# Who issues the transfers: SyncE alone, or SyncE, ScalarE and GpSimd

## The chip, the core and the metric

The kernel runs on one core of a Trainium2 chip. A core has five engines with an instruction queue each: TensorE (PE in the profile; its weight loads are PEld), VectorE (DVE), ScalarE (ACT), GpSimd (POOL) and SyncE (SP). They share an on-chip memory of 128 partitions; matmul results go to a second one, PSUM, here used as four buffers p0 to p3. Transfers are issued from the queue of SyncE, ScalarE or GpSimd and are carried out by 16 DMA engines. Each queue is worked off in program order: an instruction that has to wait holds up all that stand behind it on the same engine.

The metric is the device time of one execution in microseconds (us). Before the change it is 249.68 us, the median of three runs (249.4 to 249.89).

## The reference, cut to what matters

Two layers, each of them a sequence mixer A (a long convolution over the sequence with a gate) and an MLP B. The mixer's kv and its convolution depend on k, v and the filter alone, so both layers use the same y, and the kernel computes it once.

```python
def _A_ref(q, k, v, shift_k, ssm_k, ssm_D):      # S = 2048, D = 512
    k_shift = ...                                # 4 taps along the sequence
    kv = k_shift * v
    y = irfft(rfft(kv, 2S) * rfft(ssm_k, 2S))[:S]  # long convolution
    y = y + kv * ssm_D
    return q * y

def _B_ref(x, w1, b1, w2, b2):                   # 512 -> 1376 -> 512
    return gelu(layernorm(x) @ w1 + b1) @ w2 + b2

x = A_q
x = x + _A_ref(layernorm(x), A_k, A_v, A_shift_k, A_ssm_k, A_ssm_D)
x = x + _B_ref(layernorm(x), B_w1, B_b1, B_w2, B_b2)
x = x + _A_ref(layernorm(x), A_k, A_v, ...)      # the second layer
x = x + _B_ref(layernorm(x), ...)
return x
```

## The kernel before: the parts that the change touches

The kernel is a list of pieces, and a table ORDER that says in which order they are emitted and on which engine each runs: `sw00.S` puts the piece sw00 on SyncE, `.A` is ScalarE, `.G` GpSimd, `.D` VectorE, `.P` TensorE; digits name the buffers taken. The order within an engine is the order in this table.

The convolution is done as matrix products on a two-step transform. K pieces transform the filter, kv pieces are the taps, U pieces the first transform step of kv, X the second, T the product with the filter's spectrum (on VectorE), V and Y the way back. Then come the gate, the layer norms and the MLPs (m1, ge, m2, ad), one group of tokens after the other.

The filter's spectrum lies in two copies, the second with the two halves of the partitions swapped. The half swaps (sw00, sw01, sw10, sw11: first digit the half of the features, second the half of the frequencies) write the second copy with two transfers each:

```python
def swap(it, off=off):                                   # line 421
    for a in range(2):
        queue(it).dma_start(at(KSW + off, [[1, 16 * 256]], a, 64, 2), at(off, [[1, 16 * 256]], 1 - a, 64, 2))
KX[f].append(add(f"sw{f}{j}", {"S": 1200}, deps, swap, dma=2700))
```

A product T reads both copies, so T00 and T01 need sw00, T02 and T03 need sw01, T20 and later ones sw10 and sw11:

```python
def mul(it, xe=xe, spec=spec):                           # line 513
    eng = nc.vector if it["eng"] == "D" else nc.gpsimd
    xb = view(xbb[xe["slot"]["xb"]], [8, CW])
    x2 = apf(xb, xb.offset, [list(xb.ap[0]), [0, 2], [CW, 8], [1, CW]])
    eng.tensor_tensor(spec(), x2, spec(), ALU.mult)      # line 517
tm = add(f"T{cc}{j}", {"D": 1140}, [xe, KX[cc // 2][j // 2]] + KW[cc // 2][2 * j:2 * j + 2], mul,
         free=[(xe, "xb")])
```

The loads and the transposes. A piece's queue follows from its letter; the transposes by DMA always go to SyncE:

```python
def queue(it):
    return {"S": nc.sync, "A": nc.scalar, "G": nc.gpsimd}[it["eng"]]

def load(name, dst, src, ns, deps=(), after=()):
    return add(name, {"S": 400, **QUEUE.get(name, {})}, deps, lambda it: queue(it).dma_start(dst, src), dma=ns, after=after)   # line 325

def ktload(ct):                                          # k, transposed: line 369
    return lambda it: nc.sync.dma_start_transpose(kT[:, ct, 16:16 + S], k_d[:, ct * P:ct * P + P])
lv = [load(f"lv{o}", uv[:, 8 * o:8 * o + 8, :], vd[:, 8 * o:8 * o + 8, :], 2650) for o in range(2)]
lW = load("lW", Wt[:], W_h.ap().bitcast(BF16), 2650)     # transform tables
lM = load("lM", Mt[:], M_h.ap().bitcast(BF16), 5300)
...
lx = load("lx", xr[:], qd[:, GT:NT, :], 4000, s1p)       # x of groups 1 to 3
w1 = load("w1", W1t[:], B_w1.rearrange("(ct p) f -> p ct f", p=P), 3600)

def w2load(it):                                          # lines 546 to 548
    queue(it).dma_start(W2t[:, 0:FT - 1, :], ...)
    queue(it).dma_start(W2t[0:FL, FT - 1, :], ...)
    queue(it).dma_start(W2t[FL:FL + 1, FT - 1, :], apf(B_b2, 0, [[D, 1], [1, D]]))
```

GpSimd computes the first layer norm's statistics of group 0 (piece pa00, lines 622 to 636; its scratch lies where W1 will be, so w1 waits for it), then the power -1/2 of them (pb0, lines 273 and 275). Later it applies that norm (pc00, pc01, line 284), sets a row of ones (ho, line 553) and computes more such powers.

TensorE has two groups of 28 matmuls on the identity: one at the start (`warm`, line 97) and one in a wait ahead of the MLP (`IDLE = (28, 0, 0)`, line 670).

Of the kernel before, what the change touches and what calls it, by code (L numbers as in the profile page):

```python
# [14 lines left out]

ORDER = """
warm.P dg.D lK1.S lK0.S lK3.S lv1.S lH.S lx0.S lk0.S KT1.P0 KT1e.D KT0.P1 K1S0.P2 KT0e.D K1S3.P3 K1S0e.A0 K1S2.P0
K1S3e.D K0S3.P1 K1S2e.A K0S0.P2 K0S0e.D1 K1S1.P3 K0S3e.A KT3.P0 K1S1e.A K0S1.P1 lv0.S KT3e.D K0S2.P2 pa00.G lK2.S
K0S1e.A K1T1.P3 lW.S K0S2e.D lM.S lk3.S K3S0.P0 K3S3.P1 K3S0e.A2 K1T1e.D K0T1.P2 K3S3e.A K3S1.P0 K0T1e.D K1T0.P3
K3S1e.A K0T0.P1 K1T0e.D kv0.P20 K0T0e.D K3S2.P3 kvm01.D KT2.P1 K3S2e.A kvm00.D K3T0.P3 KT2e.A U0S0.P0 K3T0e.D K3T1.P2  # L20
U0S0e.A3 K200.P1 K3T1e.D U0S1.P3 K200e.A K201.P0 U0S1e.D K205.P2 K201e.A U0S2.P1 K205e.A U0S2e.D K207.P3 K2S0.P0
K207e.A U0S3.P2 K2S0e.D4 K2S1.P1 lk1.S U0S3e.A K2S2.P3 K2S3.P0 K2S2e.D K2S1e.A U0T0.P2 K2S3e.A K202.P1 U0T0e.D5
K204.P3 K202e.A K2T1.P0 K204e.D K203.P2 lk2.S U0T1.P1 K2T1e.D K203e.A X00.P3 pb0.G U0T1e.D K2T0.P2 X00e.A0 K216.P0
K2T0e.D sw00.S K217.P1 K216e.A K214.P3 K217e.D K211.P2 K214e.A w1.S K215.P0 K211e.A K215e.D K210.P1 K206.P3 K210e.A
K212.P2 K206e.D sw11.S X01.P0 K212e.A X03.P1 X01e.D1 X02.P3 sw01.S X03e.A2 K213.P2 K213e.A T00.D kv2.P01 sw10.S T01.D
X02e.A0 kv1.P23 kvm21.D kvm20.D kvm11.D U2S0.P0 V00.P1 U2S0e.A6 kvm10.D V00e.A0 U2S3.P0 U2S3e.D U1S0.P2 U1S1.P3
U1S0e.A1 U1S2.P1 U1S1e.D U2S1.P0 U1S2e.A U1S3.P2 T02.D U2S2.P3 U1S3e.A V01.P1 U2S1e.D U2S2e.A U1T0.S2 V02.P2 V01e.D
kv3.P30 V02e.A U1T1.S T03.D V03.P1 kvm31.D pc00.G U2T0.S3 V03e.A kvm30.D X10.P2 X10e.A1 X11.P1 U3S1.P0 pc01.G X11e.A0
# [2 lines left out]
T21.D X22e.A2 X23.P0 X23e.A0 V11e.D V20.P1 V13e.A V21.P0 T22.D TP00.S6 V20e.A3 X30.P3 T23.D X31.P2 X30e.A1 V22.P1  # L31
X31e.D2 V21e.A V23.P3 TP01.S V22e.A T30.D X33.P0 X32.P2 V23e.A TP11.S T31.D Y00.P1 X32e.A0 V30.P3 Y00e.D TP02.S
X33e.A1 Y01.P2 T32.D V31.P1 Y01e.A TP12.S T33.D V30e.A4 V32.P0 V31e.A ga0.D V33.P2 TP21.S V32r.A Y02.P3 V32f.D ho.G
V33f.A gs0.D lx.S Y02e.A TP03.P1 TP30.S V33r.A ga1.D TP03e.A TP13.P0 TP23.P3 gs1.D TP13e.A Y03.P2 TP33.P1 gl0.D
TP23e.A Y11.P0 gl2.D gp0.G TP33e.A Y10.P3 gb0.D Y11e.A gp2.G gl1.D LT0.P1 TP20.S LT0e.A gb2.D gp1.G Y10e.A m10x0.P0
Y03e.D gb1.D pa10.D LT1.P1 ge0x0.A m10x1.P2 TP31.S LT2.P3 LT1e.D pa21.D m10y0.P1 TP32.S LT2e.A pa11.D ge0x1.A m10y1.P0
TP22.S ge0y0.A m10z0.P3 pa20.D w2.S pb1.G m10z1.P2 ge0y1.A pc10.D ge0z0.A pb2.G pc11.D m10z2.P1 pd10.D ge0z1.A Y30.P0
pd11.D ge0z2.A Y20.P3 Y21.P2 Y20e.A pe10.D Y31.P1 pc21.A m200.P3 pe11.D Y31e.A Y21e.A pa30.D pf1.G pc20.A pg11.D
pg10.A pd20.D lt11.S m201.P1 Y30e.A pd21.D lt10.S pe20.D pe21.D m110.P2 ad01.D pf2.G m111.P0 ge10.A pa31.D pg21.A
m112.P1 pg20.D pb3.G ge11.A pa41.D lt21.S m113.P2 ge12.A lt20.S pc30.D m114.P0 pc31.D ge13.A pd30.D m115.P1 ge14.A  # L40
# [751 lines left out]
```

## Time and profile before

| | |
|---|---|
| Time | 249.68 us (249.4 to 249.89) |
| Span of the profiled execution | 247.7 us |
| ScalarE's share, GpSimd's share | 59%, 20% |
| Moved by the DMA engines | 31.06 MB, 54778 packets |
| Of it on SyncE's queue (q1) | 30.68 MB, 49.5% of 16 engines' span |
| On ScalarE's queue (q10), on GpSimd's (q0) | 0.07 MB, 0.00 MB |
| Half swaps: issue to landing, min, median, max | 3.0, 7.2, 7.8 us |
| k transposes: issue to landing, min, median, max | 5.7, 10.9, 15.1 us |

How to read it: part 2 of the page cuts the span into 40 slices of 6.2 us, and a digit is the busy share of an engine in tenths. A row of a timeline has the start in us, the time taken in us, engine, line, operation, what is written and read, and a count; a q behind the engine's name means its queue, that is, the issue of a transfer and not its data. The time to issue is not the time to move: when a transfer has landed is told by the updates of its semaphore. In the names, low and high are the two large blocks of on-chip memory, so low<-low is a half swap, high<-tabM the table M, Wt<-tabW the table W.

### The profile page before, as it was taken

Reading aid. Unit: us, or ns where it says so; the run is one execution under the profiler, and the core shown is the slowest. Engines: PE = TensorE matmul, PEld = TensorE weight load, DVE = VectorE, ACT = ScalarE, POOL = GpSimd, SP = SyncE. Lnnn points to the kernel's source line nnn. Section 1 sums busy time; section 2 is a strip of 40 time slices with the busy share of each in tenths; the row PEclk is TensorE's granted clock in tenths of the full one; section 3 lists DMA queues with packets and bytes.
Section 4 is the critical chain, followed back from the end, with each engine's and each line's share of the span. In section 5 each row is a group of like instructions: output and inputs, shape, how many; then the busy total and the mean of one; then the engine's idle time right before and its main releaser. Section 6 shows DMA issues by size and latency. Waiting matters only on the chain.

```text
span 247.7 us, 4836 instructions
## 1 busy us (share of the span) xinstructions
PE 235.8 (95%) x1932; PEld 148.0 (60%) x1943; DVE 174.3 (70%) x343; ACT 147.0 (59%) x214; POOL 50.3 (20%) x79
## 2 busy tenths in 40 slices
PE   7999999998998889999999999999999999999994
PEld 6899798787897688444444444444444444444443
DVE  1898899998999899999978569759659410110232
ACT  2666979478999889947787464164275264064000
POOL 4089981103001214104030110110110100000000
PEclk9999999999999999999999999999999999999999
DMA  6999999959999996041304220500400330020111
GB/s 221 328 308 443 200 264 343 423 103 178 220 187 168 285 165 228 1 85 21 67 2 84 46 43 0 77 9 3 80 5 0 68 105 0 0 85 3 42 70 57
DMA packets 54778, 31.06 MB, mean 125 GB/s; under 512 B 49410, under 2 KB 51684, under 8 KB 53604
## 3 DMA queue, kind: packets, MB, share of 16 engines
q1 hardware_dynamic: 54002, 30.68, 49.5%
q8 instruction: 15, 0.25, 0.4%
q0 software_dynamic: 80, 0.00, 0.3%
q10 hardware_dynamic: 674, 0.07, 0.2%
q14 instruction: 7, 0.06, 0.1%
HBM read 12.40 MB, written 2.10 MB: 59 GB/s over the span
## 4 chain that ended last, share of the span: by engine, by line
PE 73%; DVE 12%; ACT 8%; DMA 4%; issue 2%; DVEq 0%; ACTq 0%
PE p_89 L748 10%; PE p_90 L748 9%; PE p_90 L722 8%; PE p_88 L722 8%; PE p_89 L722 8%; PE p_91 L748 7%; PE p_91 L722 6%; PE p_88 L748 5%; DVE low L336 3%; DMA ZT_83<-ZT_80 2%; PE p_88 L347 2%; DMA sT<-in_A_shift_k_dram 2%; ACT xb_84 L334 2%; DVE low L517 1%; PE p_91 L403 1%
## 5 line engine op out<-in xcount | busy, mean ns | idle before, releaser
L722 PEld LDWEIGHTS <-W1t 128*128 128x128 bf16 (+1 forms) x440 | 40.2, 100 | 37.5 <-issue 1.4
L748 PEld LDWEIGHTS <-low 128*128 128x128 bf16 (+1 forms) x363 | 35.4, 98 | 40.8
L748 PE MATMUL p_89<-low 128*128 128x512 bf16 (+3 forms) x119 | 25.9, 369 | 0.1
L733 ACT ACTIVATE low<-p_88,B_72 128x512 bf16<-128x512 f32 (+3 forms) x33 | 17.1, 588 | 14.8 <-PE p_89 L748 10.3
L756 DVE TENSOR_TENSOR high<-p_90,high 128x1024 bf16<-128x1024 f32 (+1 forms) x5 | 5.6, 1118 | 28.4 <-PE p_90 L748 28.4
L722 PE MATMUL p_88<-low,W1t 128*128 128x512 bf16 (+3 forms) x132 | 23.7, 326 | 0.7 <-ACT low L334 0.7
L733 ACT ACTIVATE low<-p_90,B_72 128x512 bf16<-128x512 f32 (+4 forms) x28 | 15.9, 639 | 11.7 <-PE p_90 L722 8.5
L722 PE MATMUL p_90<-low,W1t 128*128 128x512 bf16 (+4 forms) x112 | 22.7, 347 | 0.0
L748 PE MATMUL p_90<-low 128*128 128x512 bf16 (+1 forms) x95 | 22.0, 379 | 0.2
L733 ACT ACTIVATE low<-p_89,B_72 128x512 bf16<-128x512 f32 (+4 forms) x29 | 14.9, 593 | 11.8 <-PE p_91 L748 9.0
L722 PE MATMUL p_89<-low,W1t 128*128 128x512 bf16 (+4 forms) x116 | 20.6, 324 | 0.4 <-DVE low L336 0.4
L748 PE MATMUL p_91<-low 128*128 128x512 bf16 (+1 forms) x76 | 17.2, 379 | 0.1
L722 PE MATMUL p_91<-low,W1t 128*128 128x512 bf16 (+2 forms) x80 | 17.2, 358 | 0.0
L733 ACT ACTIVATE low<-p_91,B_72 128x512 bf16<-128x512 f32 (+2 forms) x20 | 11.8, 655 | 7.0 <-PE p_89 L748 3.1
L525 PEld LDWEIGHTS <-low 128*128 128x128 bf16 x256 | 15.0, 98 | 1.2 <-issue 0.7
L748 PE MATMUL p_88<-low 128*128 128x512 bf16 (+2 forms) x64 | 13.6, 361 | 0.1
L756 DVE TENSOR_TENSOR high<-p_89,high 128x1024 bf16<-128x1024 f32 (+1 forms) x5 | 5.3, 1062 | 9.3 <-PE p_89 L748 9.3
L606 DVE TENSOR_TENSOR high<-high 128x1024 bf16<-128x1024 bf16 (+1 forms) x16 | 10.7, 669 | 1.2 <-ACT high L286 1.1
L263 DVE BATCH_NORM_STATS2 lst_104<-high 128x6 f32<-128x512 bf16 x16 | 10.2, 682 | 0.1
L263 DVE BATCH_NORM_STATS2 lst_96<-high 128x6 f32<-128x512 bf16 x16 | 10.2, 680 | 0.0
L627 POOL TENSOR_TENSOR W1t<-W1t 128x512 f32<-128x512 f32 (+8 forms) x17 | 9.7, 568 | 1.3
L273 POOL TENSOR_TENSOR lrs_98<-lrs_98,mhalf 128x4 f32<-128x4 f32 x4 | 4.0, 1006 | 27.5 <-DVE lnm_99 L270 27.5
(227 smaller groups left out, 446.6 us busy)
## 6 DMA issues: line engine op xcount, KB each, us to landing
low<-low SPq DMA_DIRECT2D x8, 512.0 KB, 7.2
low<-in_A_ssm_k_dram SPq DMA_DIRECT2D x4, 512.0 KB, 5.0
high<-in_A_v_dram SPq DMA_DIRECT2D x2, 1024.0 KB, 7.5
high<-tabM SPq DMA_DIRECT2D x1, 2048.0 KB, 14.0
high<-in_A_q_dram SPq DMA_DIRECT2D x1, 1536.0 KB
W1t<-in_B_w_dram SPq DMA_DIRECT2D x1, 1376.0 KB
low<-in_B_w_dram SPq DMA_DIRECT2D x1, 1280.0 KB, 6.7
Wt<-tabW SPq DMA_DIRECT2D x1, 1024.0 KB, 8.4
```

What stands on the lines that cost most here:

```text
L263: nc.vector.bn_stats(self.st[:, i, h, :], xg(g, i, i + 1, c0, c9)[:, 0, :])
L273: nc.gpsimd.tensor_tensor(self.rs[:, a:b], self.rs[:, a:b], mhalf[:, a:b], ALU.pow)
L334: nc.scalar.activation(d, s, AF.Copy)
L336: nc.vector.tensor_copy(d, s)
L347: nc.tensor.matmul(o[:, i, :], src[:, 4 * q + i, cs], Ft[:], start=True, stop=not extra)
L525: nc.tensor.matmul(o[:, i, :], T[:, r, i, :], Mt[:, k0 + i, r, :], start=r == 0, stop=r == 1)
L606: nc.vector.tensor_tensor(tmp[:, a:b, c0:c9], ln[:, a:b, c0:c9], ys, ALU.mult)
L627: g_.tensor_tensor(d[:, :, 0:w], src[:, :, 0:w], src[:, :, w:2 * w], ALU.add)
L722: nc.tensor.matmul(o[0:m, ft - fts[0], :], W1t[:, ct, ft * P:ft * P + m], lnT[n % 3][:, a:b, ct, :], start=ct == 0, stop=ct == CT - 1)
L733: nc.scalar.activation(hT[n % 2][0:m, ft, a * P:b * P], psv(pe, dims)[0:m, ft - fts[0], :], AF.Gelu_apprx_tanh, bias=B1[0:m, ft:ft + 1])
L748: nc.tensor.matmul(o[:, i - a, 0:c9 - c0], hT[n % 2][0:m, ft, i * P:(i + 1) * P], W2t[0:m, ft, c0:c9], start=ft == 0, stop=ft == FT - 1)
L756: nc.vector.tensor_tensor(xs, psv(pe, [2, D])[:, 0:b - a, 0:c9 - c0], xs, ALU.add)
```

## The change

Nothing is computed differently and nothing is moved otherwise; only the queue from which some transfers are issued changes. In the table ORDER, v's second load half (lv0), W and M go from SyncE to ScalarE; the four half swaps (eight transfers), W1, x of groups 1 to 3 and W2 go from SyncE to GpSimd. All transposes by DMA, the other loads and the stores stay with SyncE. Both groups of identity matmuls are in both kernels. The aim is that SyncE, in whose queue the transposes stand, is not held up by plain transfers.

```diff
-K1S3e.D ... K1S1e.A K0S1.P1 lv0.S KT3e.D K0S2.P2 pa00.G lK2.S
-K0S1e.A K1T1.P3 lW.S K0S2e.D lM.S lk3.S K3S0.P0 ...
+K1S3e.D ... K1S1e.A K0S1.P1 lv0.A KT3e.D K0S2.P2 pa00.G lK2.S
+K0S1e.A K1T1.P3 lW.A K0S2e.D lM.A lk3.S K3S0.P0 ...
...
-K2T0e.D sw00.S K217.P1 K216e.A ... K214e.A w1.S K215.P0 ...
-K212.P2 K206e.D sw11.S X01.P0 ... X02.P3 sw01.S X03e.A2 K213.P2 K213e.A T00.D kv2.P01 sw10.S T01.D
+K2T0e.D sw00.G K217.P1 K216e.A ... K214e.A w1.G K215.P0 ...
+K212.P2 K206e.D sw11.G X01.P0 ... X02.P3 sw01.G X03e.A2 K213.P2 K213e.A T00.D kv2.P01 sw10.G T01.D
...
-V33f.A gs0.D lx.S Y02e.A TP03.P1 TP30.S ...
+V33f.A gs0.D lx.G Y02e.A TP03.P1 TP30.S ...
...
-TP22.S ge0y0.A m10z0.P3 pa20.D w2.S pb1.G ...
+TP22.S ge0y0.A m10z0.P3 pa20.D w2.G pb1.G ...
```

(Cut: the lines are shortened at the three dots; all letters that change are shown.) On GpSimd sw00 comes after pa00 and pb0, and w1, sw11, sw01 and sw10 follow it in this order, ahead of pc00; lx comes after ho, w2 ahead of pb1. On ScalarE lv0 comes after K1S1e, and lW and lM come after K0S1e, ahead of K3S0e.

More of the change, by code (lines that the diff above doesn't have):

```diff
@@ L17 @@
 warm.P dg.D lK1.S lK0.S lK3.S lv1.S lH.S lx0.S lk0.S KT1.P0 KT1e.D KT0.P1 K1S0.P2 KT0e.D K1S3.P3 K1S0e.A0 K1S2.P0
-K1S3e.D K0S3.P1 K1S2e.A K0S0.P2 K0S0e.D1 K1S1.P3 K0S3e.A KT3.P0 K1S1e.A K0S1.P1 lv0.S KT3e.D K0S2.P2 pa00.G lK2.S
-K0S1e.A K1T1.P3 lW.S K0S2e.D lM.S lk3.S K3S0.P0 K3S3.P1 K3S0e.A2 K1T1e.D K0T1.P2 K3S3e.A K3S1.P0 K0T1e.D K1T0.P3
+K1S3e.D K0S3.P1 K1S2e.A K0S0.P2 K0S0e.D1 K1S1.P3 K0S3e.A KT3.P0 K1S1e.A K0S1.P1 lv0.A KT3e.D K0S2.P2 pa00.G lK2.S
+K0S1e.A K1T1.P3 lW.A K0S2e.D lM.A lk3.S K3S0.P0 K3S3.P1 K3S0e.A2 K1T1e.D K0T1.P2 K3S3e.A K3S1.P0 K0T1e.D K1T0.P3
 K3S1e.A K0T0.P1 K1T0e.D kv0.P20 K0T0e.D K3S2.P3 kvm01.D KT2.P1 K3S2e.A kvm00.D K3T0.P3 KT2e.A U0S0.P0 K3T0e.D K3T1.P2
@@ L23 @@
 K204.P3 K202e.A K2T1.P0 K204e.D K203.P2 lk2.S U0T1.P1 K2T1e.D K203e.A X00.P3 pb0.G U0T1e.D K2T0.P2 X00e.A0 K216.P0
-K2T0e.D sw00.S K217.P1 K216e.A K214.P3 K217e.D K211.P2 K214e.A w1.S K215.P0 K211e.A K215e.D K210.P1 K206.P3 K210e.A
-K212.P2 K206e.D sw11.S X01.P0 K212e.A X03.P1 X01e.D1 X02.P3 sw01.S X03e.A2 K213.P2 K213e.A T00.D kv2.P01 sw10.S T01.D
+K2T0e.D sw00.G K217.P1 K216e.A K214.P3 K217e.D K211.P2 K214e.A w1.G K215.P0 K211e.A K215e.D K210.P1 K206.P3 K210e.A
+K212.P2 K206e.D sw11.G X01.P0 K212e.A X03.P1 X01e.D1 X02.P3 sw01.G X03e.A2 K213.P2 K213e.A T00.D kv2.P01 sw10.G T01.D
 X02e.A0 kv1.P23 kvm21.D kvm20.D kvm11.D U2S0.P0 V00.P1 U2S0e.A6 kvm10.D V00e.A0 U2S3.P0 U2S3e.D U1S0.P2 U1S1.P3
@@ L33 @@
 X33e.A1 Y01.P2 T32.D V31.P1 Y01e.A TP12.S T33.D V30e.A4 V32.P0 V31e.A ga0.D V33.P2 TP21.S V32r.A Y02.P3 V32f.D ho.G
-V33f.A gs0.D lx.S Y02e.A TP03.P1 TP30.S V33r.A ga1.D TP03e.A TP13.P0 TP23.P3 gs1.D TP13e.A Y03.P2 TP33.P1 gl0.D
+V33f.A gs0.D lx.G Y02e.A TP03.P1 TP30.S V33r.A ga1.D TP03e.A TP13.P0 TP23.P3 gs1.D TP13e.A Y03.P2 TP33.P1 gl0.D
 TP23e.A Y11.P0 gl2.D gp0.G TP33e.A Y10.P3 gb0.D Y11e.A gp2.G gl1.D LT0.P1 TP20.S LT0e.A gb2.D gp1.G Y10e.A m10x0.P0
 Y03e.D gb1.D pa10.D LT1.P1 ge0x0.A m10x1.P2 TP31.S LT2.P3 LT1e.D pa21.D m10y0.P1 TP32.S LT2e.A pa11.D ge0x1.A m10y1.P0
-TP22.S ge0y0.A m10z0.P3 pa20.D w2.S pb1.G m10z1.P2 ge0y1.A pc10.D ge0z0.A pb2.G pc11.D m10z2.P1 pd10.D ge0z1.A Y30.P0
+TP22.S ge0y0.A m10z0.P3 pa20.D w2.G pb1.G m10z1.P2 ge0y1.A pc10.D ge0z0.A pb2.G pc11.D m10z2.P1 pd10.D ge0z1.A Y30.P0
 pd11.D ge0z2.A Y20.P3 Y21.P2 Y20e.A pe10.D Y31.P1 pc21.A m200.P3 pe11.D Y31e.A Y21e.A pa30.D pf1.G pc20.A pg11.D
```

## The prediction, made before the changed kernel was run

> **What bounds the kernel now.** I read the busy shares and the 40 slices of the page first, then engine tables by 5 us, then the timelines of SyncE, GpSimd, VectorE and ScalarE. From the page's parts 1 and 2:
>
> ```profile
> PE 235.8 (95%) x1932; PEld 148.0 (60%) x1943; DVE 174.3 (70%) x343; ACT 147.0 (59%) x214; POOL 50.3 (20%) x79
> PE   7999999998998889999999999999999999999994
> DVE  1898899998999899999978569759659410110232
> DMA  6999999959999996041304220500400330020111
> ```
>
> A slice is 6.2 us. From slice 15 on, about 91 us (where the chain of waits has the first long run of MLP matmuls), TensorE is dense to the end and nothing there waits on a transfer: that part is a block of fixed length, and what the change does to the time is what it does to the start of that block. Before it, VectorE and the transfers are busy together. The table by 5 us (busy of PE, weight loads, DVE, ACT, POOL; clock; DMA share; GB/s):
>
> ```profile
> 15.00:20.00 5.00, 5.00 (x95) 4.85 (x94) 4.26 (x4) 2.50 (x3) 4.18 (x11) 1.00 1.00 390
> ...
> 35.00:40.00 5.00, 4.81 (x52) 4.04 (x50) 4.94 (x5) 4.69 (x6) 2.77 (x9) 1.00 1.00 340
> 40.00:45.00 5.00, 4.81 (x93) 4.40 (x91) 4.98 (x6) 3.52 (x4) 0.00 (x0) 1.00 1.03 400
> 45.00:50.00 5.00, 4.45 (x56) 3.65 (x54) 4.78 (x5) 2.86 (x3) 0.77 (x1) 1.00 0.98 405
> 50.00:55.00 5.00, 4.90 (x82) 4.51 (x82) 5.00 (x5) 3.91 (x5) 0.00 (x0) 1.00 0.42 85
> ```
>
> From 35 to 55 us VectorE works 19.7 of 20 us. Its order is fixed in the program, so a wait that appears in it there is a loss of the same size. The transfers are at their limit from 36 to 52 us. They are the eight half swaps and W1, and the products T on VectorE need the swaps. SyncE's timeline (start, time to issue):
>
> ```profile
> 5.33 7.39 SPq L369 DMA_TRANSPOSE high<-in_A_k_dram  x1
> 12.77 0.57 SPq L325 DMA_DIRECT2D high<-in_A_v_dram  x1
> 13.38 0.43 SPq L325 DMA_DIRECT2D low<-in_A_ssm_k_dram  x1
> 13.86 0.43 SPq L325 DMA_DIRECT2D Wt<-tabW  x1
> 14.33 1.17 SPq L325 DMA_DIRECT2D high<-tabM  x1
> 15.54 18.16 SPq L369 DMA_TRANSPOSE high<-in_A_k_dram  x3
> 34.23 1.18 SPq L423 DMA_DIRECT2D low<-low  x2
> ```
>
> A plain transfer costs SyncE 0.4 to 1.2 us; a transpose occupies it until the transfer ahead has nearly landed. The first of the three at 15.54 us takes 12.52 of the 18.16 us, to 28.06, and M lands at 28.31. The landings (last update of each semaphore in the trace) are: v (second half) 18.55, W 22.30, M 28.31, k transposes 30.63, 34.35 and 35.95; sw00 37.22 and 38.60, W1 43.23, sw11 44.46 and 47.06, sw01 48.30 and 49.53, sw10 50.76 and 51.99. The readers on VectorE's timeline are T00 and T02 (the rows of L517), and GpSimd's timeline shows when it could issue:
>
> ```profile
> 41.39 1.22 DVE L517 TENSOR_TENSOR low<-xb_84,low 128x2048 bf16<-128x2048 bf16 x1
> ...
> 50.87 1.21 DVE L517 TENSOR_TENSOR low<-xb_84,low 128x2048 bf16<-128x2048 bf16 x1
> ```
>
> ```profile
> 29.82 6.63 POOL L627 TENSOR_TENSOR W1t<-W1t 128x1024 f32<-128x1024 f32 x9
> 37.02 1.04 POOL L273 TENSOR_TENSOR lrs_102<-lrs_102,mhalf 128x4 f32<-128x4 f32 x1
> 38.14 0.20 POOL L275 TENSOR_TENSOR lnm_103<-lnm_103,lrs_102 128x4 f32<-128x4 f32 x1
> ```
>
> The reader is to see the two margins of the swaps: T00 starts 41.39 - 38.60 = 2.79 us after the first swap has landed, T02 only 50.87 - 49.53 = 1.34 us after sw01. And GpSimd is at its statistics until 38.34, while SyncE issued the first swap at 34.23.
>
> [...] the share is 1.0 from one queue already, so no bandwidth is to be won. [...] Before has only two tiny GpSimd transfers (issues of 1.19 and 0.58 us, landing 7.4 and 6.8 us after), in a crowded start[...]. [...] VectorE's instructions here are 1.2 us long. [...] In the first 3 us of the trace SyncE and ScalarE issue side by side in 0.4 to 0.55 us each, which does not look like waiting for each other, but no transpose was being issued there.
>
> **Part by part.** The instructions of TensorE and VectorE and their order are the same; so are both groups of 28 identity matmuls, which stand in both kernels. Only issuers change.
>
> 1. v (second half), W, M go to ScalarE. Priced by SyncE's rows: 0.57 + 0.43 + 1.17 = 2.17 us of ScalarE's queue, between 12.4 and 15.6 us. ScalarE idles 0.16 us before 12.56 and 1.06 us before 14.64, so 2.17 - 1.22 = 0.95 us remain. They delay the filter stage up to 1 us, since TensorE needs the buffers that ScalarE empties. Data: v and W start about when they did and need 2 x 2.5 us (gap of such landings), so they land before their readers at 20.3 and 24.1 us. On the path at 40 us: at most +1.0.
>
> 2. k transposes. SyncE no longer stands behind M, so the three may be issued up to 12 us earlier. But their first readers, the tap matmuls of kv2 and kv1 at 41.5 and 43.4 us, wait for none of them now, and the engines must still move the same bytes, M included, by about 36 us. Worth 0.
>
> 3. First swap. SyncE issued it at 34.23; GpSimd comes to it at 38.34. The first landing took 3.0 us from issue, with 1.7 us of it behind the last k transpose (35.95 - 34.23). Now nothing is ahead, but a GpSimd issue takes perhaps 0.6 to 1.2 us[...], so I keep 3.0: 41.4, and 1.38 us more for the second half: 42.8. T00 moves from 41.39 to about 42.9, +1.5. It contains the 1.0 of step 1: the swap's time hangs on the statistics, not on ScalarE, and the later of the two counts.
>
> 4. The chain of swaps. From 38.60 the queue needs 49.53 - 38.60 = 10.9 us to the landing of sw01, at 330 to 400 GB/s. It cannot be made shorter, and the DMA engines now idle from 36 to 39 us. So sw01 lands at 42.8 + 10.9 = 53.7, T02 starts at 53.8: 53.8 - 50.87 = +2.9. This replaces the +1.5, as T02 comes after T00 on VectorE.
>
> 5. The last swap lands at 42.8 + (51.99 - 38.60) = 56.2. The first U transpose (issued at 52.00, landed 56.42, used at 56.47) shares the engines with it until then. If it makes all its way after 56.2, at the 2.3 us of the k transpose behind M (30.63 - 28.31), it lands at 58.5; its reader is at 56.47 + 2.9 = 59.4. Worth 0.
>
> 6. From T02 to the MLP block VectorE or ScalarE works without a gap of more than 0.8 us (VectorE 55 to 60 us; ScalarE from 57 to 79 us full), so nothing is caught up. The other moved loads: x (SyncE at 78.83, GpSimd at 78.3, after its memsets) lands at 86.15 before its reader at 88.87; two late transposes no longer stand 5.2 us behind it, but their readers come at 98 us. W2 is issued some 3 us earlier than SyncE's 91.09 and is needed at 101.9. Worth 0.
>
> Sum: 249.68 + 2.9 = 252.6 us.
>
> **Rivals.** (a) A free SyncE pays: the 12.5 us row speaks for it; that the taps wait on no transfer speaks against. It would need swaps as early as before, and makes 249. (b) The swaps' margin holds, GpSimd's first landing being quick and the chain shorter without transposes ahead: T02 late by 0.5 or less, 250. (c) [...] a wait of 4 us at 14 us is 4 to 5 us on the filter stage and swallows step 4, 254. The 12.5 us row shows how long such an issue can last; against it, only one plain transfer of 512 KB now stands ahead of the transpose. (d) [...] up to 1.2 us for each of the seven issues before sw01's end, 3 to 5 us beyond step 4, and 256 to 258. For it: VectorE at 98% just there[...].
>
> **Range and chances.** All but (a) and (b) give a loss; the sum of 2.9 is 1.2%. 2% is 5.0 us, a line that (c) touches and (d) crosses. Low is (b) or (a), 249.6; high is (d), 257.5. Faster by 2% would need 5 us out of a stage whose VectorE has 0.3 us of idle: 0.03. Slower by 2%: 0.27. Within: 0.70.
>
> **What would show it.** Right: a wait of VectorE on the swaps' transfers ahead of L517 at about 41 to 43 and again near 51 to 54 us; GpSimd's first swap at 38.3 us; a gap in the DMA share from 36 to 39; the MLP block starting 3 us later and as long as before. Step 1 is wrong if ScalarE's rows show issues of over 1.2 us; step 3 if T00 starts by 41.5; step 4 if the landings of the swaps are closer than 1.2 us or further apart than 1.4. The prediction falls if the first MLP run starts at or before 91.0 us, or if the block itself changes length.

## The result, and the profile after

The changed kernel takes 252.07 us (median of 4 runs, 251.93 to 253.06), the kernel before 249.59 us beside it (249.4 to 249.89): a ratio of 1.0107, with a 95% interval of 1.0079 to 1.0135. The change costs about 2.5 us. The span of the profiled execution goes from 247.7 to 250.3 us.

Parts 1 and 2 of the page after, the rows that were shown of before:

```profile
PE 237.1 (95%) x1932; PEld 148.6 (59%) x1943; DVE 174.6 (70%) x343; ACT 147.1 (59%) x214; POOL 58.2 (23%) x92
PE   7998999798999879999999999999999999999994
DVE  2896998988999999999978749759668510110232
DMA  6999946999999999040404130410210240020111
```

The same work is done in the same busy time; GpSimd's 50.3 us have become 58.2, because its 13 new issues, 7.9 us in all, count as busy there. The new thing is the two lower DMA digits at slices 5 and 6 (31 to 44 us), where there was a row of nines. The table by 5 us says more (PE, weight loads, DVE, ACT, POOL, clock, DMA share, GB/s):

```profile
15.00:20.00 5.00, 5.00 (x94) 4.85 (x93) 4.37 (x4) 2.61 (x3) 4.25 (x10) 1.00 0.98 397
...
35.00:40.00 5.00, 4.81 (x55) 4.08 (x53) 4.94 (x5) 4.38 (x6) 4.16 (x11) 1.00 0.12 51
40.00:45.00 5.00, 4.58 (x78) 4.13 (x76) 3.93 (x5) 3.64 (x5) 3.57 (x7) 1.00 0.96 334
45.00:50.00 5.00, 3.61 (x64) 3.34 (x64) 5.00 (x5) 2.01 (x3) 0.77 (x1) 1.00 1.02 371
50.00:55.00 5.00, 4.71 (x49) 3.73 (x49) 4.36 (x5) 4.59 (x5) 0.00 (x0) 1.00 0.90 374
```

From 35 to 40 us the DMA engines moved 340 GB/s before and now 51, that is, they stand nearly idle. VectorE pays in the two stretches in which it was full: 3.93 of 5 us at 40 to 45 (4.98 before) and 4.36 at 50 to 55 (5.00 before). Who was late is seen on GpSimd's timeline, and who waited on VectorE's, line 517:

```profile
37.78 0.20 POOL L275 TENSOR_TENSOR lnm_103<-lnm_103,lrs_102 128x4 f32<-128x4 f32 x1
38.34 1.22 POOL L423 DMA_DIRECT2D low<-low  x2 [0.35 <-issue]
39.55 0.81 POOL L325 DMA_DIRECT2D W1t<-in_B_w_dram  x1
```

```profile
43.54 1.22 DVE L517 TENSOR_TENSOR low<-xb_84,low 128x2048 bf16<-128x2048 bf16 x1 [1.07 <-issue]
...
53.45 1.23 DVE L517 TENSOR_TENSOR low<-xb_84,low 128x2048 bf16<-128x2048 bf16 x1 [0.45 <-DMA low<-low]
```

GpSimd ends its statistics and issues the first swap at 38.34 us (SyncE did at 34.23). By the updates of the semaphores its halves land at 41.29 and 43.46, and T00 starts at 43.54, 2.15 us later than before. The page's "issue" after the 1.07 us names no releaser; that it was the swap is seen from the landing 0.08 us earlier. W1 lands at 48.50, sw11 at 49.71 and 50.95, sw01 at 52.20 and 53.43, and T02 starts 0.02 us after that, 2.58 us later than before. (Fifteen of the 16 DMA engines are done with sw01 at 52.45 us, the last one 0.98 us later. Before, the last one was 1.37 us behind, but T02 came later still.)

SyncE's timeline is where the change was to help:

```profile
5.07 7.27 SPq L369 DMA_TRANSPOSE high<-in_A_k_dram  x1
12.38 0.57 SPq L325 DMA_DIRECT2D low<-in_A_ssm_k_dram  x1
13.00 19.30 SPq L369 DMA_TRANSPOSE high<-in_A_k_dram  x3
```

The three k transposes occupy SyncE for 19.30 us in place of 18.16. The first of them alone takes 14.23 us, to 27.23, and M, now in ScalarE's queue, lands at 27.50: SyncE stands behind M as before, although M is no longer in its queue. The three land at 29.70, 32.49 and 35.91 us, against 30.63, 34.35 and 35.95.

ScalarE's timeline, where three issues were added, and from the chain of waits the pieces that were not in it before (start, length, what):

```profile
12.68 1.02 ACT L356 ACTIVATE ZT_78<-p_89 128x1024 bf16<-128x1024 f32 x1 [0.15 <-PE p_89 L347]
12.68 0.33 ACTq L325 DMA_DIRECT2D Wt<-tabW  x1
13.06 0.44 ACTq L325 DMA_DIRECT2D high<-tabM  x1
14.76 1.02 ACT L356 ACTIVATE ZT_79<-p_88 128x1024 bf16<-128x1024 f32 x1 [1.06 <-PE p_88 L347]
```

```profile
12.38 9.40 DMA low<-in_A_ssm_k_dram
21.83 1.22 PE p_89 L387 x16
...
42.38 11.05 DMA low<-low
...
93.42 1.95 PE p_89 L722 x32
```

The issues of W and M lie beside an ACTIVATE that is running: ScalarE pays nothing for them; its rows are 0.12 us later than before, as they were ahead of the issues (8.75 against 8.63). But the chain now has a transfer of the filter, block lK2, which SyncE still issues, at 12.38 (13.38 before). It lands at 21.79 (19.84 before), and the matmuls of KT2 that need it (line 387) start at 21.83 instead of 20.59. TensorE's row of that line, before and after:

```profile
20.59 1.15 PE L387 MATMUL p_89<-IDt,low 128*128 128x128 bf16 x16
21.83 1.22 PE L387 MATMUL p_89<-IDt,low 128*128 128x128 bf16 x16 [0.96 <-DMA low<-in_A_ssm_k_dram]
```

The last row of the chain is its first long MLP run: 93.42 us, against 91.01 before.

One more loss lies behind it. The last two transposes (line 577), before and after, and what TensorE waited for in the changed kernel at line 598, where it uses them:

```profile
87.35 3.69 SPq L577 DMA_TRANSPOSE low<-ZT_80  x2
90.34 7.86 SPq L577 DMA_TRANSPOSE low<-ZT_80  x2
```

```profile
its engine sat idle before it (us, times) until:
  DMA low<-ZT_80: 0.5, 1
```

Before, they land at 91.75 and 93.01 us, 5.3 us ahead of the first row of line 598 (98.27). Now W2, which GpSimd issues at 90.26, shares the DMA engines with them: from 93 to 95 us W2's queue moves 170 packets and theirs none. They land at 99.25 and 101.65, and the reader that waits for the second starts at 101.69. From the first MLP product m1 (line 722, first row) to m2 (line 748) it takes 14.83 us in place of 14.44. Thus the loss along the way: +2.15 us at T00, +2.58 at T02, +2.19 at m1 (89.47 against 87.28), +2.58 at m2 (104.30 against 101.72), +2.6 at the end.

### The profile page after: what moved, and what is told of

It reads as the page before. It is cut to its first block, busy times and chain, and to the rows that moved or that the text cites. A ratio compares the mean times of both kernels' runs of the same rounds, so it can differ in the third digit from the quotient of the medians.

```text
span 250.3 us, 4850 instructions
## 1 busy us (share of the span) xinstructions
PE 237.1 (95%) x1932; PEld 148.6 (59%) x1943; DVE 174.6 (70%) x343; ACT 147.1 (59%) x214; POOL 58.2 (23%) x92
## 4 chain that ended last, share of the span: by engine, by line
PE 66%; DMA 10%; DVE 9%; ACT 8%; SPq 3%; issue 1%; POOL 1%; ACTq 0%; DVEq 0%
PE p_89 L748 10%; PE p_90 L748 8%; PE p_90 L722 8%; PE p_88 L722 8%; PE p_89 L722 8%; PE p_91 L748 7%; PE p_91 L722 6%; PE p_88 L748 5%; DMA low<-low 4%; DMA low<-in_A_ssm_k_dram 4%; SPq L369 3%; DVE low L336 2%; DMA sT<-in_A_shift_k_dram 2%; ACT xb_85 L334 1%; ACT xb_84 L334 1%
```

## The experiments

Each is a small edit of ORDER in the kernel before or in the changed kernel. T00, T02 and so on are starts in the profiled execution; before they are 41.39 and 50.87 us, KT2 20.59, m1 87.28, m1 to m2 14.44 us. Lines of ORDER are cut to the token that moves. The runs came in three groups, each with the kernel before on the same chip: 249.37 us for the first four, 249.21 for the second, 249.16 for the last. The ratios are not the quotients of the medians given here; they differ from them by up to 0.0012.

**ScalarE's share alone (e1).** From the kernel before:

```diff
- lv0.S   lW.S   lM.S
+ lv0.A   lW.A   lM.A
```

> The kernel before with only v (second half), W and M moved to ScalarE. Theory: ScalarE loses nothing by issuing, but the filter's third block (lK2), alone on SyncE's queue, shares the DMA engines with v and lands at about 21.8 instead of 19.8 us; its transposes on TensorE wait 1 us, and as the swaps stay with SyncE, all of it comes through: +1.0, 250.6 us. Rival A (all of the change's loss is GpSimd's swaps): 249.6. Rival B (ScalarE pays for its issues, 1 to 2 us): 251 or more, with ScalarE's rows near 12 to 15 us later than before.

Measured 250.32 us, ratio 1.0048 (1.0032 to 1.0063). lK2 lands at 21.98, KT2 starts at 22.03, T00 at 42.58, T02 at 52.05; m1 to m2 is 14.45. The 1.0 us is real, and it comes in TensorE's wait for lK2.

**The same with lK2 ahead of v in ScalarE's queue (e10).**

```diff
- lv0.S   lK2.S   lW.S   lM.S
+ lK2.A lv0.A   lW.A   lM.A
```

> Kernel before with v (second half), W and M on ScalarE, and the filter block lK2 on ScalarE too, ahead of v. Theory: issuing costs ScalarE nothing, and the loss of the same move without lK2 (1.0 us) came from lK2's sharing the DMA engines with v and W from another queue; in one queue lK2 lands by 20 us, TensorE's wait ahead of KT2 goes, T00 and T02 start within 0.3 us of before, and the time is 249.4. Rival: ScalarE's four issues cost what was estimated, some 1 us, and the time is 250.4 with KT2 on time.

Measured 249.16 us, ratio 1.0004 (0.9994 to 1.0014). KT2 starts at 20.66 with no wait. VectorE's rows of line 517, the first wait gone from both:

```profile
41.46 2.35 DVE L517 TENSOR_TENSOR low<-xb,low 128x2048 bf16<-128x2048 bf16 x2
50.93 1.22 DVE L517 TENSOR_TENSOR low<-xb,low 128x2048 bf16<-128x2048 bf16 x1
```

Four issues from ScalarE cost nothing; where lK2 stands is worth the whole 1.0 us. Even here nothing is won: the first k transpose is issued at 12.45 us, and the second, issued at 17.91, holds SyncE for 11.02 us, past M's landing (27.66).

Why a transfer in another queue holds up SyncE, and lK2, is seen in the packets. The queues of the changed kernel from 20 to 25 us, while M flows in ScalarE's queue (q10) and a k transpose waits in SyncE's (q1): packets, MB, share of 16 engines:

```profile
q10 hardware_dynamic: 145, 2.06, 98.3%
q1 hardware_dynamic: 142, 0.04, 3.6%
```

The counts are nearly the same, 145 to 142, as if the two queues took turns packet by packet, but one from ScalarE's queue has 14 KB on average (2.06 MB / 145) and one from SyncE's some 0.3 KB. When the transposes have the engines alone, from 28 to 33 us, they make 4013 packets in 5 us, 28 times as many. From 16 to 19 us it is 115 packets and 0.81 MB of v against 116 and 0.38 MB in SyncE's queue, which holds lK2 (4 KB packets): lK2, which stood in v's queue before, gets the smaller half. As the counts are nearly equal in both stretches, the queue with the smaller packets moved less in the same time, and the transpose, with the smallest, almost nothing (0.04 of 2.12 MB).

**The swaps and W1 alone by GpSimd (e2).** From the kernel before:

```diff
- sw00.S   w1.S   sw11.S   sw01.S   sw10.S
+ sw00.G   w1.G   sw11.G   sw01.G   sw10.G
```

> The kernel before with only the half swaps and W1 moved to GpSimd. Theory (the latest of several waits counts, they do not add): T00 starts at 43.5, T02 at 53.4 us, as in the changed kernel: +2.5, 252.1 us, although lK2 lands as before. Rival (the waits add up, 1.0 of the loss being lK2's): 251.1 us.

Measured 253.19 us (252.56 to 255.08), ratio 1.0154 (1.0123 to 1.0184). That the parts add up (251.1) is refuted, but the loss is even larger than expected. The profile is that of the slowest of the four executions, 255.08. In it the first swap is issued at 38.55 and lands at 41.49 and 45.14; 15 of the 16 engines are done with the second half at 43.69. The queues from 42 to 45.2 us:

```profile
q0 software_dynamic: 193, 1.05, 95.6%
q8 instruction: 1, 0.02, 2.9%
```

One 16 KB packet of instructions took 2.9% of 16 x 3.2 us, 1.5 us. That it was on the late engine is inferred, as the profile does not name a packet's engine; but it fits all 14 profiles. Each has such a packet between 42.1 and 46.1 us, and the transfers that land after it are 0.7 to 1.9 us later on their last engine than on the other 15. In the changed kernel it comes at 45.56, after the first swap; only here (42.13) and in e4 (43.43) does the swap's second half have to wait for it. VectorE then waits longest, and TensorE with it (windows; the clock is the sixth value after the stretch's length):

```profile
45.22 2.36 DVE L517 TENSOR_TENSOR low<-xb,low 128x2048 bf16<-128x2048 bf16 x2 [4.07 <-issue]
```

```profile
44.00:45.00 1.00, 0.00 (x0) 0.00 (x0) 0.00 (x0) 0.00 (x0) 0.00 (x0) 1.00 1.00 415
45.00:46.00 1.00, 0.00 (x0) 0.00 (x0) 0.78 (x1) 0.00 (x0) 0.00 (x0) 0.92 1.09 369
46.00:47.00 1.00, 0.00 (x0) 0.00 (x0) 1.00 (x2) 0.46 (x1) 0.00 (x0) 0.50 0.99 220
47.00:48.00 1.00, 0.39 (x8) 0.39 (x9) 1.00 (x2) 0.56 (x1) 0.00 (x0) 0.50 0.95 386
...
52.00:53.00 1.00, 1.00 (x14) 1.00 (x13) 1.00 (x2) 0.82 (x1) 0.15 (x1) 0.67 1.09 459
```

TensorE has no matmul for 4.2 us (43.41 to 47.61). Its granted clock falls to 0.5 at 45.83, 2.4 us into this gap, and stays there for 6.8 us. In e4's profile it falls to 0.5 after 3.5 us without a matmul; in the changed kernel, whose longest gap there is 1.2 us, it stays 1.00. Where the limit lies is not shown. The other three executions of e2 have a mean clock of 0.993, those of the kernel before and of the changed one 0.998 to 1.0. By estimate, 0.007 x 250 us / 0.5, that is up to 3.5 us at half clock in each of them. So e2 seems to lose a second time, by the clock, in all four executions; where the clock fell in the other three, and whether a packet of instructions was in the way there, is not shown. T02 then starts at 56.65, 2.2 us after sw01 has landed: it is no longer a transfer that holds it.

**lK2 first, in the changed kernel (e4).**

```diff
- lv0.A   pa00.G lK2.S
+ lK2.A lv0.A   pa00.G
```

> The changed kernel with lK2 on ScalarE ahead of v. Theory: the wait for lK2 at 21 us is gone, the filter stage is 1.0 us earlier, but sw00's landing hangs on GpSimd's statistics: T00 still at 43.5, time as the changed kernel, 252.1 us. Rival (waits add up): 251.1 us.

Measured 253.5 us (252.26 to 254.96), ratio 1.0177 (1.0129 to 1.0225). KT2 starts at 20.78 without a wait, and the time does not fall: the two losses overlap, and the later one counts. But the time is higher than expected. The profile, again of the slowest execution, shows what e2's did: the first swap complete at 45.46 (15 engines at 43.91), TensorE idle for 4.0 us, the clock at 0.74 from 45 to 50 us. Of the four executions only the one of 252.26 us has a mean clock of 1.0 (the others 0.991 to 0.993), and it alone is near the expected 252.1. The wait for lK2 in the changed kernel even has a good side: TensorE comes 1.2 us later to the swap's wait, its gap stays short, and all eight executions of it have a mean clock of 0.998 or more.

**The first swap back on SyncE (e3).** In the changed kernel:

```diff
- sw00.G
+ sw00.S
```

> The changed kernel with the first swap sw00 back on SyncE. Theory: sw00 is issued at about 35.2 and landed by 39.6 us, T00 waits for no transfer, the rest of the chain has time, and only lK2's 1.0 us is left: 250.6 us. Rival (transfers issued by GpSimd are slower as such, so the chain up to sw01 is still late): T02 at 53 us or later, 251.7 us or more.

Measured 250.9 us, ratio 1.0072 (1.0056 to 1.0089). sw00 is issued at 35.48 and lands at 38.41 and 39.65; T00 starts at 42.64 with no wait on it, T02 at 52.12. T00's wait was the late issue by GpSimd. What remains at T00, 1.25 us, is lK2's delay (KT2 at 22.09); another 0.3 us goes between m1 and m2 (14.76).

**Less work for GpSimd ahead of the swap (e7).** The changed kernel without the second tree of sums in GpSimd's statistics (the variance of group 0 isn't summed, so its norm is another one):

```diff
         g_.tensor_tensor(d[:, :, :], d[:, :, :], d[:, :, :], ALU.mult)
-        total(d)
```

> The changed kernel, leaving out the second tree of sums in GpSimd's statistics (the variance of group 0 is then not summed), so that GpSimd is free at 31.5 instead of 38.2 us. Theory: the first swap is issued as soon as its data are there, about 35.3 us, lands by 40, T00 does not wait, lK2's 1.0 us is left: 250.6 us. Rival (the GpSimd path is slow, whenever it starts): T00 at 43 us or later, 251.7 us or more.

Measured 250.52 us, ratio 1.0056 (1.0038 to 1.0073). GpSimd now waits for the swap's data instead of being behind:

```profile
35.34 1.22 POOL L423 DMA_DIRECT2D low<-low  x2 [3.95 <-ACT low L334]
36.56 0.81 POOL L325 DMA_DIRECT2D W1t<-in_B_w_dram  x1
```

The swap lands at 38.30 and 40.45, T00 starts at 42.23, T02 at 51.71, with no wait on a transfer. GpSimd's path is not slow (2.96 us from issue to the first landing; 2.93 for SyncE's in e3); it came late, because GpSimd had other work.

**Both remedies (e5).** The changed kernel with sw00 on SyncE and lK2 first:

```diff
- lv0.A   lK2.S   sw00.G
+ lK2.A lv0.A   sw00.S
```

> The changed kernel with sw00 on SyncE and lK2 on ScalarE ahead of v. Theory: both causes gone, nothing else in the change costs: 249.6 us, the same as before. Rival (x, W2 or GpSimd's other issues cost as well): 250.2 or more.

Measured 250.5 us, ratio 1.0059 (1.004 to 1.0078): the theory is refuted, 1.3 us are still missing. T00 starts at 41.43, as before. But T02 starts at 51.57, since sw01 lands only at 51.49: W1, ahead of it in GpSimd's queue, is issued only at 37.94, when GpSimd's statistics are done; SyncE did it at 36.77 in the kernel before. And the last transposes land at 97.78 and 100.16; m1 to m2 is 15.11 us.

**W1 behind the swaps (e6).** In the changed kernel:

```diff
- w1.G sw11.G sw01.G sw10.G
+ sw11.G sw01.G sw10.G w1.G
```

> The changed kernel with W1 issued after the last swap instead of after the first. Theory: sw01 lands 5 us earlier (W1 took 43.46 to 48.50), so T02 does not wait; T00 still does: +2.15 instead of +2.58, 251.7 us. Rival (the chain is not what holds T02): 252.1 us.

At a mean clock of 0.999 and 1.0 its executions took 252.34 and 252.98 us, ratio 1.0138 (1.0116 to 1.016); two more, at 0.991 and 0.935, took 257.31 and 290.01 us. sw01 lands at 49.90, and T02 starts at 52.32 without a wait: W1's 5 us were what held T02. The first swap's second half also lands earlier, 1.48 us after the first instead of 2.17, so T00 starts at 42.94 rather than 43.54. The win is lost again soon: m1 starts at 89.44, as in the changed kernel (89.47), for TensorE's matmuls of line 506 wait 1.3 us in all for their transposes (0.2 in the changed kernel). W1, which now lands at 56.66, stands beside the first of these. Then TensorE waits for the last transpose (landed at 102.66), and m1 to m2 is 15.87. So the time is no better than the changed kernel's, against the theory's 251.7.

**x and W2 alone by GpSimd (e8).** From the kernel before:

```diff
- lx.S   w2.S
+ lx.G   w2.G
```

> The kernel before with only x and W2 moved to GpSimd. Theory: no reader waits, 249.6 us; the last two transposes ahead of the MLP land later, near 99 us, because W2 flows at the same time, within 0.3 us of their readers. Rival (they are late, or x is): 250 or more, with a wait of TensorE on L598 or of VectorE on L263.

Measured 249.32 us (12 runs, 248.91 to 252.15), ratio 1.0016 (0.9992 to 1.004). By the median this part alone costs nothing, as expected. But single executions take 250 to 252 us, and the profiled one (250.5) shows why: m1 to m2 is 15.84, with the last transpose landing at 100.18 and its reader at line 598 starting at 100.27. The margin of 5 us is used up; what is left is so little that it differs from one execution to the next.

**x and W2 back on SyncE (e12), and the changed kernel again (e9).** In the changed kernel:

```diff
- lx.G   w2.G
+ lx.S   w2.S
```

> The changed kernel with x and W2 back on SyncE. Theory: the first MLP product m1 starts 2.2 us later than before, as in the changed kernel, but the last two transposes no longer share with W2, land by 97 us, and m1 to m2 is 14.4 us: 251.7 us, 0.4 below the changed kernel. Rival: the 0.4 us had another cause, and it stays at 252.1.

> The changed kernel once more, beside the other runs of this call. Theory: the first swap's late issue (+2.2 us at T00, +2.6 at T02, 0.4 of it made up, 0.4 lost again at the last transposes) makes about 252.1 us, T00 at 43.5, and TensorE keeps its full clock. Rival: the landing of the first swap varies with an instruction fetch on one DMA engine, as in the two runs in which it came at 45.1 and 45.5 us; then T00 starts near 45.3 here too, the granted clock falls between 45 and 52 us, and the time is 253 or more.

The changed kernel again: 252.28 us (252.1 to 252.44), ratio 1.0132 (1.0108 to 1.0155); T00 at 43.78, T02 at 53.73, clock full, m1 to m2 14.84. That is 3.1 us above the kernel before in this group, against 2.5 in the first comparison. With x and W2 on SyncE: 251.57 us, ratio 1.0107 (1.0086 to 1.0128). SyncE's timeline has the order of before, the transposes and then W2:

```profile
82.59 10.55 SPq L577 DMA_TRANSPOSE low<-ZT  x5
93.19 0.59 SPq L546 DMA_DIRECT2D low<-in_B_w_dram  x1
```

The last transposes land at 94.07 and 95.10, and m1 to m2 is 14.45. W2's place is worth 0.4 us in that row, 0.7 us of the time in this comparison. That it is W2 and not x is seen from the two transposes ahead of these: they land at 92.36 and 93.23 here and at 92.51 and 93.41 in the repeat.

**What is left without the four losses (e11).** Changed kernel with lK2 ahead of v on ScalarE, and sw00, W1, x and W2 on SyncE; only sw11, sw01 and sw10 stay with GpSimd:

```diff
- lv0.A   lK2.S   sw00.G   w1.G   lx.G   w2.G
+ lK2.A lv0.A   sw00.S   w1.S   lx.S   w2.S
```

> Of the change only v, W, M (with lK2 ahead of them) by ScalarE and the swaps sw11, sw01, sw10 by GpSimd are left; the first swap, W1, x and W2 are issued by SyncE. Theory: no late first swap, no filter block in competition, no W1 between GpSimd's swaps, no W2 beside the last transposes: every known cost is out, so T02 waits for no transfer, m1 to m2 is 14.4 us as before, and the time is 249.4. Rival: spreading transfers over three queues costs by itself about 1 us somewhere in the middle, whatever stands in which queue: 250.5.

Measured 249.22 us (20 runs), ratio 1.0006 (0.9998 to 1.0013).

```profile
41.21 2.35 DVE L517 TENSOR_TENSOR low<-xb,low 128x2048 bf16<-128x2048 bf16 x2
50.68 1.22 DVE L517 TENSOR_TENSOR low<-xb,low 128x2048 bf16<-128x2048 bf16 x1
```

With sw01 landed at 48.58, T02 waits for nothing; m1 to m2 is 14.45. Spreading transfers over three queues cost nothing here by itself, and gained nothing. The four losses (lK2's place, the late first swap, W1 ahead of sw01, W2 beside the last transposes) are the whole account, and no version here beats the kernel before.

## Why the prediction was right, and where it was not

252.6 us were predicted, 252.07 measured, and 252.28 in the repeat; as a loss, 2.9 us against 2.5 and 3.1. The sum holds, and its main term, the late first swap and the chain behind it, for its own reason. Parts of three steps (1, 2 and 6) were wrong, and it is partly luck that their errors are small.

- **Step 1 failed.** "0.95 us remain" for ScalarE: it is 0. The issues are shorter than SyncE's (0.35, 0.33 and 0.44 us) and lie beside running ACTIVATEs; e10 has all of them, lK2's too, and the time of before. Yet the filter stage did lose its 1.0 us, for a reason that the step had not asked for: lK2, left alone in SyncE's queue, shares the engines with v's larger packets (116 packets and 0.38 MB to 115 and 0.81 MB from 16 to 19 us). "v and W land before their readers" was right and looked at the wrong transfer. As the step had said of its own term, the loss is swallowed by the swap's wait (e4).
- **Step 2 was right that it is worth 0, and wrong that the transposes "may be issued up to 12 us earlier".** The first is issued 2.5 us earlier (13.00 against 15.54) and keeps SyncE until M has nearly landed. That is the aim of the change, and it fails at this point: M left SyncE's queue, but it flows on the same engines, and SyncE's transpose ends at 27.23 us, M at 27.50.
- **Step 3, mechanism right, a term too small.** Issue at 38.34 and first landing at 41.29, against 38.34 and 41.4. But "1.38 us more for the second half" measured 2.17 (2.15 in the repeat, 1.48 in e6, where W1 doesn't follow at once). T00 moves by 2.15 in place of 1.5. e3 and e7 show the cause from both sides.
- **Step 4, right.** The idle DMA engines at 35 to 40 us, the landings 1.22 to 1.25 us apart, T02 starting at sw01's landing. The chain took 53.43 - 43.46 = 9.97 us in place of 10.9. Of the difference 0.4 us is the last engine, 0.98 us behind in place of 1.37; the rest fits W1's having had part of its way by then. So T02 moved by 2.58, not 2.9.
- **Step 5, right that nothing is lost there.** The first U transpose, issued at 54.05, landed at 59.10 and not at 58.5; its reader starts at 59.15, 2.68 us later than before. The margin of 0.05 us is that of the kernel before (56.42 and 56.47).
- **Step 6, one half open, one half wrong.** "Nothing is caught up": from T02 to m1 it is 36.02 us, against 36.41. But e10 and e11, whose T02 starts on time, have 36.05 and 36.08. So it need not be lateness made up: in the profile of before TensorE waits 0.7 us there for a transpose (line 587). "W2 worth 0": the step asked when W2 is needed and not what it passes. In SyncE's queue it stood behind the last transposes; from GpSimd it comes beside them: they land 5.2 and 6.6 us later than in e12, and TensorE loses 0.4 us. The prediction had named a change in the length of the MLP block as a sign against it, and that sign came: TensorE does wait for a transfer there.

Of the rivals, (a) failed by step 2; the swaps' margin of (b) did not hold; a wait of ScalarE beside SyncE's transpose (c) isn't there: M is issued in 0.44 us at 13.06, just after SyncE has begun its transpose of 14.23 us. (The "0.4 to 0.55 us each" at the start overlooks one issue of SyncE's, of 0.76 us at 2.79.) Longer issues of GpSimd beside a busy VectorE (d) were not seen: each of its swap issues takes 0.52 to 0.65 us, next to a VectorE that is busy 79% to 99% of the time. The 4 us of (c) and the 1.2 us an issue of (d) were the author's estimates; no run shows either.

## What to carry to other kernels

Before a transfer is moved to another queue, ask two things: when does the new engine come to it, and which transfers did the old order let pass first. A queue was also a priority here: with lK2 ahead of v in one queue KT2 started at 20.66 us (e10), with the two in different queues at 22.03 (e1); and a transpose beside a plain load from another queue nearly stood still (142 packets in 5 us, the load 145 of 14 KB). With the DMA engines full from one queue (a share of 1.00 at 15 to 20 us and at 35 to 40 before), a second and a third queue gained no time here even where every known loss was taken out (e10, ratio 1.0004; e11, 1.0006).

## What was not expected of the hardware

- Transposes beside a plain transfer from another queue: 142 packets in 5 us against 4013 alone. SyncE, which issued them, was held for that time too (14.23 us for one issue).
- ScalarE issued a transfer in 0.33 to 0.49 us while an ACTIVATE of 1.02 to 1.04 us ran, and its next one wasn't later (14.76 us in the changed kernel, whose rows were 0.12 us late already ahead of the issues, and 14.38 in e10; 14.64 before).
- One 16 KB packet of instructions and one of 16 engines that was 1.45 us behind the others at a transfer's completion (e2) go together. In both profiles that showed this at the first swap TensorE's gap grew to 4 us and its clock fell to 0.5, for 6.8 and 3.4 us: in e2 2.4 us after the last matmul, in e4 3.5 us.
- With little or nothing ahead, GpSimd's and SyncE's transfers took the same 2.9 to 3.0 us from issue to landing (GpSimd's at 38.34 in the changed kernel 2.95 us, its first packet 1.2 us after the issue, and in e7 2.96; SyncE's at 35.48 in e3 2.93).
